# Recurrent attention and a Strassen-tiled MLP: one transfer per seventh of w_out, block 1's turns behind the step, the last output's sums inside its last products

## The chip, the cores and the metric

The kernel runs on one NeuronCore of a Trainium2 chip. The metric is device time in microseconds (us) of one execution; a figure given for a kernel is the median of several executions, and all outputs are float32.

## The reference

Attention in its recurrent form feeds a two-layer MLP with the quick-GELU gate:

```python
# q, k, v: (4, 8, 768, 64)
for t in range(S):
    state = gamma * state + einsum('bhd,bhe->bhde', k[:, :, t], v[:, :, t])
    y[:, :, t] = scale * einsum('bhd,bhde->bhe', q[:, :, t], state)
x = y.transpose(0, 2, 1, 3).reshape(3072, 512)
h = x @ w_in                                # 512 x 2048
g = h * (1.0 / (1.0 + exp(-1.702 * h)))
out = g @ w_out                             # 2048 x 512
```

gamma is one constant per head. The weights arrive as float64 words and are narrowed to float32 on the chip.

## The kernel before

**Blocks.** The 3072 rows are worked in six blocks (`for m in range(NB)`) of 512. Attention runs in 24 chunks of 64 time steps for two batches each; four chunks make the x of a block. Chunk j is made by three functions. `turn(j)` brings its q and k into the transposed form (from chunk 8 on by VectorE's transposes, L251) and then starts the loads of chunk j + 2 (16 transfers on SP's queue, L154). `step(j, f)` lets TensorE work on chunks j and f at once: L287 multiplies k and q of chunk j into `pa`, L295 makes the state's update, L304 and L310 the output `py` of chunk f. VectorE then masks `pa` into `at` (L316), updates the state (L366), makes `tmp` (L328) and the block's x in `X` or `X1` (L345); POOL scales k into `kd` (L272) and ages the state (L357). `pa` and `py` have one buffer each, so a step can't start before VectorE has read the step before.

**Products.** `up` makes h from x and w_in, `down` and `down49` make the output from g and w_out. Matrix products follow the Strassen-Winograd scheme: seven products of half-size quarters instead of eight, with sums of quarters before and after. Blocks 0 and 1 use this once for w_out (`down`, matmuls on L684: 28 units `n`, eight recorded matmuls each, of seven products with four units). Blocks 2 to 5 use it once in `up` (L469) and twice in `down49` (L572): each of the seven products is again seven products of quarters of quarters, here called the seven inner products of each *seventh*.

**What is prepared during blocks 0 and 1.** While TensorE works on blocks 0 and 1, the other engines make the sums that later blocks need:
- `inner_w2(i)`, VectorE, once per seventh i: three sums of w_out's quarters (L519) into `X[:, 4]`, `X[:, 5]`, `X[:, 6]`, each built on the one before, and for each a transfer on SP's queue (L520) into the DRAM tile `W2D[i]`, from where `stream` (L541) brings them back on POOL's queue in blocks 2 to 5. All seven sevenths use the same three slots of X, so a slot can be written again only when its transfer has read it. These slots hold part of block 0's g before, and the sums of x for block 2 after: `sums_x` (POOL, L440 to L443) makes `X[:, 4]`, `X[:, 6]`, `X[:, 5]` and `X[:, 2]` at the end of block 1, and the third product of `up` reads `X[:, 5]`.
- `inner_w2_t3` (L525), one more sum per seventh, in place.
- `sums_w1` (POOL, L432 to L435), sums of w_in; two tiles of 1792 KB of them leave on SP's queue to DRAM (L437, `W1D`).
- `sums_g(m, p)`: VectorE's L456, L457, L458 and POOL's L459 make sums of g between the third and the fourth product of `down`; the fourth product (units 12 to 15) reads them.

**Order.** Only TensorE's order, and some early work, is kept as written. For the other engines a scheduler orders the instructions when the program is built, from the order in which they are recorded and from what they depend on; each engine and each queue then runs its own in that order, and an instruction that waits holds all behind it. In block 1 the list `between` hands one entry to the recording after every third unit: the decay of chunk 8 with the loads of k and v, then `step` 9, `turn` 10, `step` 10, `turn` 11, and so on to `step` 12, one entry each. From block 2 on an entry is a step together with the next turn.

**Outputs.** `put` (L658 in `down`, L589 in `down49`) sums a finished product with kept ones into `o` and sends it out: in `down` on POOL's queue (L661), in the last block on ACT's (L602). In `down49` each of a block's four output tiles takes a first sum for each of the two halves of a seventh's inner products (L593, 128x512 and 128x384) and four more that put the inner products together (L598 to L601). For the very last output these follow the last matmul of the kernel.

Of the kernel before, what the change touches and what calls it, by code (L numbers as in the profile page):

```python
# [9 lines left out]
F32 = mybir.dt.float32  # L10
# [3 lines left out]
P = 128  # L14
# [14 lines left out]
def kernel(  # L29
# [29 lines left out]
    pe, act, dve, pool, sp = nc.tensor, nc.scalar, nc.vector, nc.gpsimd, nc.sync  # L59
# [8 lines left out]
    CB = 4  # L68
    BT = CB * P
    TH = BT // 2  # L70
    NB = NCH // CB
# [12 lines left out]
    ps = ctx.enter_context(tc.tile_pool(name="ps", bufs=2, space=bass.MemoryType.PSUM))  # L84
# [428 lines left out]
    def inner_w2(i):  # L513

        b11, b12, b21, b22 = w2q(ORDER[i][1])
        t = []
        for k, a in enumerate((b12, b22, b21)):
            t.append(X[:, 4 + k].rearrange("p c (d e) -> p (c d) e", e=P))
            dve.tensor_sub(t[k], a, t[k - 1] if k else b11)  # L519
            sp.dma_start(W2D[i][:, k], t[k])  # L520

    def inner_w2_t3(i):

# [25 lines left out]
    def down49(m, ring, comps):  # L549

        b, t0 = m * CB // NC * 2, m * CB % NC * D
        rows = out.rearrange("(b t) (e c) -> e t b c", b=B, c=EH)[:, t0:t0 + TH, b:b + 2, :] \
            .rearrange("e (h p) b c -> h e p b c", p=P)
        own = late.tile([P, 7, 4, P], F32, name="own", tag="late1")
        acc, kept = {}, {}

        def derive(i):
            q = [G[:, u::2, ORDER[i][0], h * P:(h + 1) * P] for u in range(2) for h in range(2)]
            a11, s3, a12, s2 = q
            d = own[:, i % 2 * 3:i % 2 * 3 + 3]  # L560
            dve.tensor_add(d[:, 0], s2, a11)
            dve.tensor_sub(d[:, 1], a12, s2)
            dve.tensor_add(d[:, 2], s2, s3)
            b11, t3, b21, b22 = w2q(ORDER[i][1])
            t1, t2, t4 = [comps[i][:, k] for k in range(3)]
            return [(a11, b11), (a12, b21), (s2, t2), (s3, t3)], [(d[:, 0], t1), (d[:, 1], b22), (d[:, 2], t4)]

        def products(p0, pairs, new):
            for j in ((0, 1, 3, 2) if len(pairs) == 4 else range(3)):
                a, w = pairs[j]  # L570
                for d in range(NP // 2):
                    pe.matmul(p0[:, j, :], a[:, d], w[:, d], start=(new and j == 0 and d == 0),  # L572
                              stop=(d == NP // 2 - 1), skip_group_check=True)

        def home2(name, first, rest):
            kept[name] = first.rearrange("p (j e) -> p j e", e=P), rest[:, 0:3 * P].rearrange("p (j e) -> p j e", e=P)
            return kept[name]

        flat = X[:, 4:6].rearrange("p s c t -> p (s c t)")
        def keep(name, half):  # L580
            if half == 0:
                if name in "pt":
                    home2(name, flat[:, 0:4 * P], flat[:, 4 * P:7 * P])
                else:
                    home2(name, (own if name == "u" else ring)[:, 6].rearrange("p j e -> p (j e)"),
                          one.tile([P, 2 * EH], F32, name=name, tag="s2" if name == "u" else "s3"))
            return kept[name][half]

        def put(th, e, half, y, a):  # L589
            if half == 0:  # L590
                kept[th, e] = two.tile([P, 7, P], F32, name="o")
            c = kept[th, e]
            dve.tensor_add(c[:, 4 * half:4 + 3 * half], y, kept[a][half])  # L593
            if half == 0:
                return
            last = m == NB - 1
            eng = dve if last else pool
            eng.tensor_add(c[:, 1:3], c[:, 1:3], c[:, 0:1].to_broadcast([P, 2, P]))  # L598
            eng.tensor_add(c[:, 3], c[:, 3], c[:, 2])
            eng.tensor_add(c[:, 0:5:4], c[:, 2:4], c[:, 4:5].to_broadcast([P, 2, P]))  # L600
            eng.tensor_add(c[:, 2:4], c[:, 0:4:3], c[:, 5:7])  # L601
            (act if last else pool).dma_start(rows[th, e], c[:, 1:5].rearrange("p (b f) e -> p b (f e)", b=2))  # L602

        def then(i, half, p0):
            if i == 0:
                act.activation(keep("p", half), p0, AF.Copy)
            elif i == 1:
                put(0, 0, half, p0, "p")
            elif i == 2:
                act.activation(keep("u", half), p0, AF.Copy)  # L610
            elif i == 3:
                act.activation(keep("v", half), p0, AF.Copy)
            elif i == 4:
                u = kept["u"][half]
                dve.tensor_add(keep("t", half), p0, u)
                put(1, 1, half, p0, "v")
            elif i == 5:
                put(0, 1, half, p0, "t")
            else:
                put(1, 0, half, p0, "v")  # L620

        pairs = {}
        todo = []
        for i in range(7):
            for half in range(2):
                def unit(i=i, half=half):
                    if half == 0:
                        if i == 0:
                            pairs[0] = derive(0)
                        x = "x" if i in (0, 2, 3) else "y"  # L630
                        if i != 2 and i != 3:
                            for n in range(2):
                                acc[x, n] = ps.tile([P, 4 - n, P], F32, name="pq", tag=x)
                    x = "x" if i in (0, 2, 3) else "y"
                    products(acc[x, half], pairs[i][half], i not in (2, 3))
                    then(i, half, acc[x, half])
                    if half == 0 and i < 6:
                        pairs[i + 1] = derive(i + 1)
                    if half == 1:
                        if i + 2 < 7:  # L640
                            comps[i + 2] = stream(ring, i + 2)
                        if i in (0, 1, 3):
                            sums_g_outer((0, 1, None, 2)[i])
                todo.append(unit)
        return todo
# [189 lines left out]
    """.split():  # L835
        works[name]()
    ordered[0] = False
    def chunks(first, last):

        return [s for j in range(first, last + 1)  # L840
                for s in (lambda j=j: turn(j), lambda j=j: step(j, j - 1))]

    for m in range(NB):
        between = []
        if m == 0:
            between = [lambda: turn(2 * CB), lambda: step(2 * CB), lambda: None, lambda: None, lambda: turn(2 * CB + 1)]
        elif m == 1:
            between = [lambda: (decay(2 * CB), load(2 * CB + 1, "v"))] + chunks(2 * CB + 1, 3 * CB)[1:]
        elif 1 < m < NB - 1:
            last = min((m + 2) * CB, NCH - 1)  # L850
            for j in range((m + 1) * CB + 1, last + 1):
                between.append(lambda j=j: (step(j, j - 1), j < last and turn(j + 1)))
            if last == NCH - 1:
                between.append(lambda: step(None, NCH - 1))
        if m > 1:
            if m > 2:
                W1B[:] = [late.tile([P, 2, 7, 2, P], F32, name=f"W1B{i}", tag=f"late{i}") for i in range(2)]
                pool.dma_start(W1B[0], W1D[0])
            for d in range(NP // 2):
                up(d)  # L860
                if d == 0 and m > 2:
                    pool.dma_start(W1B[1], W1D[1])
                if d == 0 and m < NB - 1:
                    turn((m + 1) * CB + 1)
                if d == NP // 2 - 2:
                    ring = begin_ring()
                if m == 2:
                    for i in range(2 * d, min(7, 2 * d + 2)):
                        inner_w2_t3(i)
        for n, unit in enumerate(down(m) if m < 2 else down49(m, *ring)):  # L870
            unit()
            if m == 0 and n < NP and n % 2:
                sums_w2(n - 1)
            if m == 0 and NP <= n < 3 * NP // 2:
                sums_w2_t3(2 * (n - NP))
            if m == 1 and n % 8 == 3:
                sums_w1(n // 4)
            if m == 1 and n % 3 == 1 and n < 21:
                inner_w2(n // 3)
            if between and (n % 3 == 2 if m < 2 else n % 3 == 1):  # L880
                between.pop(0)()
                if m == 1 and not between:
                    sums_x()
            if 1 < m < NB - 1 and n == 11:
                sums_x()
# [46 lines left out]
```

## Time and profile before

| what | us |
|---|---|
| median of 6 executions | 675.34 |
| lowest, highest | 675.03, 676.61 |
| the profiled execution | 675.44 |
| its span, from the first to the last instruction | 673.7 |
| TensorE busy in it | 653.7 |
| VectorE busy | 442.3 |
| POOL busy | 170.7 |

The profile is one execution. Times in it count from the span's start. PE is TensorE, PEld its loading of weights, DVE VectorE, ACT ScalarE, POOL GpSimd, SP the engine that only issues transfers; a "q" behind a name is the engine's sequencer or queue. A row of a timeline gives start, length, engine, line, operation, output<-input, shapes, the number of instructions merged into it, and in brackets the idle time before it with what ended it. The share of the clock that TensorE was granted is 1.00 at full speed. A float32 matmul is recorded as two.

### The profile page before, as it was taken

The page shows a single profiled execution, that of the slowest core. Times are in us where ns is not written, and L with a number is a line of the kernel's source. Part 1 is how long each engine was busy: PE and PEld are TensorE (multiplying, and loading weights), DVE is VectorE, ACT ScalarE, POOL GpSimd, SP SyncE. Part 2 cuts the span into 40 slices and gives each one's busy share as a digit, 9 for nine tenths or more (in the row PEclk, how much of TensorE's full clock was granted, in tenths as well). Part 3 has the DMA queues.
Part 4 walks back from the last instruction along what each step waited for, and adds up shares of the span by engine and source line. Part 5 has one row for each costly group of instructions (what it writes and reads, how often), then busy time and mean ns, then how long its engine had stood idle before and what let it go on. Part 6 is the DMA issues. An engine that isn't in the chain of part 4 may idle for free.

```text
span 673.7 us, 15357 instructions
## 1 busy us (share of the span) xinstructions
PE 653.7 (97%) x6502; PEld 568.5 (84%) x6502; DVE 442.3 (66%) x613; ACT 156.7 (23%) x313; POOL 170.7 (25%) x189
## 2 busy tenths in 40 slices
PE   6799999999999899999999999999999999999996
PEld 4688864747888778888999988999988999988996
DVE  3798890879868795254986254996254995254964
ACT  5665423321000000233210233110233110233110
POOL 3000000020278241300245700255700255400000
PEclk9999999999999979999999999999999999999999
DMA  9989741332324944322177662276662243602232
GB/s 184 219 221 224 190 135 70 133 94 44 67 86 149 331 115 113 86 31 94 61 177 176 187 171 94 66 180 174 184 169 93 67 142 110 250 0 94 69 136 95
DMA packets 145493, 88.98 MB, mean 132 GB/s; under 512 B 129648, under 2 KB 130672, under 8 KB 144400
## 3 DMA queue, kind: packets, MB, share of 16 engines
q1 hardware_dynamic: 136528, 48.27, 31.1%
q0 software_dynamic: 6752, 38.42, 15.8%
q10 hardware_dynamic: 2144, 1.31, 0.7%
q8 instruction: 51, 0.84, 0.5%
q14 instruction: 18, 0.15, 0.1%
HBM read 72.37 MB, written 15.47 MB: 130 GB/s over the span
## 4 chain that ended last, share of the span: by engine, by line
PE 87%; DVE 5%; DMA 4%; issue 2%; POOL 1%; SPq 0%; ACT 0%; POOLq 0%; DVEq 0%; ACTq 0%
PE pq L572 26%; PE px L469 16%; PE py L469 12%; PE ph L425 8%; PE pd L684 8%; PE ph L412 8%; DVE X L519 2%; PE pa L287 2%; DMA W2D<-X 2%; PE py L310 2%; PE pa L295 1%; PE py L304 1%; PE pt L248 1%; DMA v_in<-in_v_dram 1%; DMA whole<-in_col_decay_dram 1%
## 5 line engine op out<-in xcount | busy, mean ns | idle before, releaser
L572 PE MATMUL pq<-W,G 128*128 128x128 f32 x672 | 80.2, 276 | 0.0
L572 PEld LDWEIGHTS pq<-W,G 128*128 128x128 f32 x672 | 77.6, 192 | 1.2 <-issue 0.7
L541 POOL DMA_DIRECT2D ring<-W2D x28 | 15.5, 554 | 232.2 <-PE px L469 121.9
L469 PE MATMUL px<-X,W1A 128*128 128x256 f32 x256 | 59.8, 379 | 0.0
L469 PE MATMUL px<-X,W1B 128*128 128x256 f32 x256 | 59.8, 379 | 0.0
L572 PE MATMUL pq<-ring,own 128*128 128x128 f32 x448 | 59.8, 276 | 0.0
L572 PEld LDWEIGHTS pq<-ring,own 128*128 128x128 f32 x448 | 54.5, 192 | 0.4
L469 PEld LDWEIGHTS px<-X,W1B 128*128 128x128 f32 x256 | 48.6, 190 | 6.6
L469 PEld LDWEIGHTS px<-X,W1A 128*128 128x128 f32 x256 | 48.4, 190 | 6.5
L684 PE MATMUL pd<-W,G 128*128 128x256 f32 x224 | 50.6, 386 | 0.0
L684 PEld LDWEIGHTS pd<-W,G 128*128 128x128 f32 x224 | 43.0, 194 | 6.2
L469 PE MATMUL py<-X,W1B 128*128 128x256 f32 x192 | 45.4, 379 | 0.0
L469 PE MATMUL py<-X,W1A 128*128 128x256 f32 x192 | 45.4, 379 | 0.0
L391 ACT ACTIVATE G<-G 128x512 f32<-128x512 f32 x48 | 30.2, 630 | 52.0 <-DVE G L479 33.3
L469 PEld LDWEIGHTS py<-X,W1B 128*128 128x128 f32 x192 | 36.5, 190 | 5.0
L469 PEld LDWEIGHTS py<-X,W1A 128*128 128x128 f32 x192 | 36.5, 190 | 5.0
L487 DVE TENSOR_TENSOR t<-py,u 128x512 f32<-128x512 f32 x16 | 11.1, 692 | 35.5 <-PE py L469 35.5
L476 ACT ACTIVATE p<-px 128x512 f32<-128x512 f32 x16 | 9.6, 597 | 96.7 <-PE px L469 96.7
L572 PE MATMUL pq<-W,own 128*128 128x128 f32 x224 | 29.6, 275 | 0.0
L572 PE MATMUL pq<-ring,G 128*128 128x128 f32 x224 | 29.6, 275 | 0.0
L501 DVE TENSOR_TENSOR G<-G 128x512 f32<-128x512 f32 (+2 forms) x24 | 12.3, 513 | 25.7 <-ACT G L391 25.7
L412 PE MATMUL ph<-X,W1A 128*128 128x256 f32 x128 | 29.1, 383 | 0.0
(196 smaller groups left out, 1185.7 us busy)
## 6 DMA issues: line engine op xcount, KB each, us to landing
ring<-W2D POOLq DMA_DIRECT2D x28, 768.0 KB, 4.9
W1B<-W1D POOLq DMA_DIRECT2D x6, 1792.0 KB, 10.3
W<-in_moe_w_in_dram SPq DMA_DIRECT2D x12, 512.0 KB, 7.1
W2D<-X SPq DMA_DIRECT2D x21, 256.0 KB, 2.8
W<-in_moe_w_out_dram SPq DMA_DIRECT2D x10, 512.0 KB, 4.2
out_dram<-o POOLq DMA_DIRECT2D x20, 256.0 KB, 3.6
v_in<-in_v_dram SPq DMA_DIRECT2D x64, 64.0 KB, 3.2
q_sq<-in_q_dram SPq DMA_DIRECT2D x128, 32.0 KB, 2.2
```

The lines of the kernel that those rows point to most:

```text
L287: pe.matmul(pa[HALF[w], u, 0, s, :], kt[HALF[u], w, s, :], qt[HALF[u], w, s, :], start=True, stop=True)
L310: pe.matmul(py[HALF[o], w, 0, 2 * u + s2 if f < 2 * CB else 2 * s2 + u, :], vn[HALF[w], HP * u + s, :], a[HALF[w], u, s, :], start=True, s ...
L391: pin(act.activation(g, h[:, i], AF.Gelu_apprx_sigmoid))
L412: pe.matmul(h[:, ab], w, X[:, 2 * th + c // 2, c % 2, :], start=(ab == 0 and c == 0), stop=(c == 3), skip_group_check=True)
L425: pe.matmul(h, w, X1[:, c // 2:4:2, c % 2, :], start=(c == 0), stop=(c == 3))
L469: pe.matmul(acc[:, u, :], t[:, q1 + u, sa, c, :], X[:, sb, c, :], start=(start and u == 0 and c == 0), stop=(stop and c == 1), skip_group_ ...
L487: dve.tensor_add(tt, z, u)
L501: dve.tensor_sub(q[0][1], q[0][0], q[0][1])
L519: dve.tensor_sub(t[k], a, t[k - 1] if k else b11)
L541: pool.dma_start(c, W2D[i])
L572: pe.matmul(p0[:, j, :], a[:, d], w[:, d], start=(new and j == 0 and d == 0), stop=(d == NP // 2 - 1), skip_group_check=True)
L684: pe.matmul(p0[:, n, :], g1(m, p, sa)[:, n * P:(n + 1) * P], W2[:, sb, p, :], start=(new and p == 0 and n == 0), stop=(last and p == NP - ...
```

## The change

It has three parts.

1. `inner_w2` makes its three sums as before and then issues one transfer of all three slots (768 KB) instead of one of 256 KB after each sum.
2. In block 1, an entry of `between` is now a step with the next turn, followed by an empty entry. The steps stay behind the same units; the turns of chunks 10, 11 and 12 are recorded right behind the step before them, three units earlier.
3. The last inner half-product of the last block goes through the new `finish`: its first product gets the old accumulator `p0`, the other two a tile `p1` of their own. The five sums that need only `p0` and kept values are recorded ahead of one last sum that needs `p1`, and the output leaves in four transfers of 64 KB, three on ACT's queue and one on SP's, each behind the sum that completes it.

The matmuls are the same, in the same order. In the built program the scheduler's order on the other engines differs in blocks 0 and 1 too: on VectorE, the mask, the state's update, the transposes of turn 10 and the step's two output sums of step 9 stand behind the fifth seventh, and three sums of the sixth seventh ahead of the sums of g; on SP, the transfers of the sixth and the seventh seventh stand behind the loads of turns 11 and 12; on POOL, the third output transfer of block 1 stands ahead of the four sums of `sums_x` instead of behind them, and `X[:, 6]` ahead of `X[:, 5]`.

```diff
@@ inner_w2
         for k, a in enumerate((b12, b22, b21)):
             t.append(X[:, 4 + k].rearrange("p c (d e) -> p (c d) e", e=P))
             dve.tensor_sub(t[k], a, t[k - 1] if k else b11)
-            sp.dma_start(W2D[i][:, k], t[k])
+        sp.dma_start(W2D[i].rearrange("p k d e -> p (k d e)"), X[:, 4:7].rearrange("p k c t -> p (k c t)"))
@@ products, in down49
-            for j in ((0, 1, 3, 2) if len(pairs) == 4 else range(3)):
+            for j in ((0, 1, 3, 2) if len(pairs) == 4 else range(len(pairs))):
@@ new, in down49
+        def finish(p0, ab):
+            c, v = kept[1, 0], kept["v"][1]
+            p1 = ps.tile([P, 2, P], F32, name="pq", tag="x")
+            products(p0, ab[:1], True)
+            products(p1, ab[1:], True)
+            at = [rows[1, 0][:, b, f * P:(f + 1) * P] for b in range(2) for f in range(2)]
+            dve.tensor_add(c[:, 1:3], c[:, 1:3], c[:, 0:1].to_broadcast([P, 2, P]))
+            act.dma_start(at[0], c[:, 1])
+            dve.tensor_add(c[:, 3], c[:, 3], c[:, 2])
+            dve.tensor_add(c[:, 4], p0[:, 0], v[:, 0])
+            dve.tensor_add(c[:, 0:5:4], c[:, 2:4], c[:, 4:5].to_broadcast([P, 2, P]))
+            act.dma_start(at[3], c[:, 4])
+            dve.tensor_add(c[:, 5:7], c[:, 0:4:3], v[:, 1:3])
+            dve.tensor_add(c[:, 2:4], p1, c[:, 5:7])
+            for n in range(2):
+                (act, sp)[n].dma_start(at[1 + n], c[:, 2 + n])
@@ unit, in down49
+                    if i == 6 and half == 1 and m == NB - 1:
+                        finish(acc[x, half], pairs[i][half])
+                        return
                     products(acc[x, half], pairs[i][half], i not in (2, 3))
@@ main loop; chunks() is removed
         elif m == 1:
-            between = [lambda: (decay(2 * CB), load(2 * CB + 1, "v"))] + chunks(2 * CB + 1, 3 * CB)[1:]
+            between = [lambda: (decay(2 * CB), load(2 * CB + 1, "v"))]
+            for j in range(2 * CB + 1, 3 * CB + 1):
+                between += [lambda j=j: (step(j, j - 1), j < 3 * CB and turn(j + 1)), lambda: None]
+            between.pop()
```

More of the change, by code (lines that the diff above doesn't have):

```diff
@@ L837 @@
     ordered[0] = False
-    def chunks(first, last):
-        return [s for j in range(first, last + 1)
-                for s in (lambda j=j: turn(j), lambda j=j: step(j, j - 1))]
     for m in range(NB):
```

## The prediction

> **What bounds the kernel now.** I read the page first, for the engine that is never idle, then the chain of waits around its one hole, then the engines' timelines there and at the end.
>
> ```profile
> span 673.7 us, 15357 instructions
> ...
> PE 653.7 (97%) x6502; PEld 568.5 (84%) x6502; DVE 442.3 (66%) x613; ACT 156.7 (23%) x313; POOL 170.7 (25%) x189
> ...
> PEclk9999999999999979999999999999999999999999
> ```
>
> TensorE is busy all through; the only dent in its clock is slice 15 (236 to 253 us), in block 1. The chain there, columns start, length, what:
>
> ```profile
> 207.92 7.31 DVE X L519
> ...
> 221.48 7.39 DMA W2D<-X
> ...
> 228.96 1.29 DVE X L519 x2
> ...
> 236.03 0.62 DVE qT L251
> 236.65 0.60 DVE kT L251
> 237.26 0.14 issue
> 237.39 1.21 PE pa L287 x25
> ```
>
> The transposes of turn 10 (L251) stood late in VectorE's order, behind the sums of w_out's quarters (L519), one of which took 7.31 us beside POOL, and a wait of 7.39 us for their transfer. TensorE idled 4.08 us, to 237.39, and then worked at half clock (window, PE, PEld, DVE, ACT, POOL busy, clock, DMA share, GB/s):
>
> ```profile
> 221.00:233.00 12.00, 12.00 (x169) 10.65 (x160) 7.22 (x11) 0.57 (x1) 2.81 (x3) 1.00 1.01 371
> ...
> 237.40:243.30 5.90, 5.90 (x133) 5.42 (x134) 5.90 (x8) 0.00 (x0) 2.86 (x3) 0.50 0.53 122
> ...
> 15.00:27.00 12.00, 7.27 (x270) 6.30 (x267) 9.15 (x16) 8.31 (x23) 0.67 (x2) 1.00 1.06 203
> ```
>
> A step takes 2.03 us elsewhere and took 3.70 here; the next 48 matmuls took 11.69 us against 10.63. The hole costs 4.08 + 1.67 + 1.06 = 6.8 us. The first window shows the transfer queue full at 371 GB/s just before. The start of block 2, on TensorE and then POOL:
>
> ```profile
> 273.86 1.89 PE L469 MATMUL px<-X,W1A 128*128 128x256 f32 x8
> ...
> 277.31 1.89 PE L469 MATMUL px<-X,W1A 128*128 128x256 f32 x8
> ```
>
> ```profile
> 270.73 1.27 POOL L442 TENSOR_TENSOR X<-X 128x512 f32<-128x512 f32 x1
> ...
> 273.30 1.72 POOL L443 TENSOR_TENSOR X<-X 128x512 f32<-128x512 f32 x1
> ```
>
> The product at 277.31 reads X[5], which L442 makes by 272.0: 5.3 us to spare. The end, on VectorE and on ACT's queue:
>
> ```profile
> 668.41 0.56 DVE L593 TENSOR_TENSOR o<-pq,v 128x384 f32<-128x384 f32 x1 [1.20 <-PE pq L572]
> 669.00 0.42 DVE L600 TENSOR_TENSOR o<-o 128x256 f32<-128x256 f32 x1
> 669.46 0.42 DVE L601 TENSOR_TENSOR o<-o 128x256 f32<-128x256 f32 x1
> ```
>
> ```profile
> 669.91 0.38 ACTq L602 DMA_DIRECT2D out_dram<-o  x1
> ```
>
> Prices of transfers (KB each, us to landing):
>
> ```profile
> W2D<-X SPq DMA_DIRECT2D x2, 256.0 KB, 2.0
> ```
>
> ```profile
> W1D<-W1B SPq DMA_DIRECT2D x1, 1792.0 KB, 6.5
> ```
>
> ```profile
> ring<-W2D POOLq DMA_DIRECT2D x28, 768.0 KB, 4.9
> ```
>
> **One transfer per seventh.** 21 issues on SP become 7; SP's time was waiting, so the 14 issues of 0.32 us saved are worth nothing. But the first sum of the next seventh rewrites X[4], which now waits for 768 KB that leave after the third sum, where it waited for 256 KB that left after the first. So sums and transfer of successive sevenths stand in series. A transfer of 768 KB is not shown from SP; between 2.0 us (256 KB) and 4.9 us (the same size read back by POOL) I take the line through 2.0 and 6.5 us: 2.0 + 512/1536 x 4.5 = 3.5 us. A sum alone follows the last by 0.70 us; beside POOL's sums of w_in it takes 1.49 to 1.76, and I take 1.65. The first seventh ends at 195.56 as before. Seventh 1: 199.1 to 204.1; 2: 207.6 to 212.5; 3: 216.0 to 220.6 (POOL's sums end near 219.8). The two 1792 KB transfers of w_in's sums follow POOL: the first enters the queue at about 216.4, ahead of seventh 3's, the second behind it, and seventh 4's behind both. From 217.2, 1.0 us after that issue (the landing of 2.0 us less its data), the queue must move 1792 + 768 + 256 (an output) + 1792 + 768 KB = 5.5 MB: at 371 GB/s 14.8 us, so the fifth transfer lands at 232.2. At the 449 GB/s of the best slices in that stretch it is 230.0; at 4.9 us a transfer, sevenths 1 to 3 are 4.2 us later and it lands near 235. Meanwhile seventh 4's sums run at about 225.1 to 227.2.
>
> **Turns behind the step.** In the changed program's order on VectorE, mask, state, both transposes of turn 10, and the step's two output sums follow seventh 4 directly: six instructions, 3.7 us, done at 230.9. TensorE asks for them at 232.9, so its wait is gone, with 2 us of cover; seventh 4 later than 229.2 brings it back. turn's loads of q and k move with it on SP: in the changed order the 16 of turn 11 (some 9 us of issues, as from 249.6 to 259.0 before, and held until its transposes near 248) stand ahead of the sixth transfer, so that this is issued near 257 and lands near 260.5. The last seventh's first sum stands in VectorE's order near 257 and holds it up to 3.5 us; behind it wait only sums due after TensorE's unit that ends near 264, so I cost this at nothing. The last transfer, behind eight loads of k and v (5.1 us) and the 16 of turn 12 (8.0), is issued near 270.5 and lands near 274.0; L440, which overwrites its source, could not start before 275 anyway (below), a cover of 1 us.
>
> What is late next are the block's own sums of G (L456 to L458), 12 instructions, which now stand behind the sixth seventh. They begin after the fifth landing and five VectorE sums: 232.2 + 5 x 0.61 = 235.3. They take 12 x 0.60, 8 dependent ones 0.1 more (0.8), and three subtractions of POOL's (L459, 1.26 less the overlap, 1.13 each: 3.4): 11.4 us, ending 246.7. TensorE's fourth unit after the step reads the last. Before, that unit began at 252.6 - 3 x 1.73 = 247.4; without any stall it would be 240.5. So of 6.8 us the stage keeps 0.7, between 2.9 (landing at 230.0) and -2.1 (235).
>
> **The start of block 2.** In POOL's order the block's third output transfer stood behind the four sums of X (L440 to L443); in the changed order it stands ahead of them, and X[5] comes third instead of second. That output is the last product of block 1. Counted from TensorE's end of the block (273.86 before): VectorE's sum ends 0.9 us later, POOL starts the issue 0.3 later (221.15 after 220.86 in the trace), 0.74 to issue, three sums 3.75: X[5] comes 5.7 us after the block's end, and its product wants it at 3.45. TensorE stalls 2.3 us. With the 0.7 kept, the stage ends 1.6 us late (-0.6 to +4.4).
>
> **The end.** Before, three VectorE sums end 1.50 us after the last matmul, at 669.88. After, the others run during the last products (L593 to 666.4, then five of 0.29 or 0.42 with 0.03 between, to 668.2) and one 128x256 sum of 0.42 is left: 668.84, 1.04 us earlier. 64 KB on each of two queues instead of 256 KB on one: 2.16 us to landing becomes 1.95 (q's 32 KB loads land in 1.9 to 2.2). Together -1.25 us, between -0.9 and -1.5.
>
> Sum: +1.6 - 1.25 = +0.35. The profiled execution took 675.44 us around its span of 673.7, 0.1 over the median of 675.34; so 675.7.
>
> [...] Before, one sum was held 7.30 us, through five POOL instructions. [...]
>
> [...] Idling of 1.80 us at 24.48 left the clock at 1.00 (third window above), 4.08 did not. Stalls of 2.3 are nearer the first, so I add nothing, and keep 3 us (half of the 5.9 us window at 0.50) as the other end.
>
> **Rivals.**
> - Exchange (forecast, chance 0.44): the hole goes, two smaller ones come, the end gains. 675.7, own range 674.2 to 676.6.
> - The queue is quick (0.26): fifth landing at 230.0 to 230.5, for which the best slices speak, against it the 371 GB/s of the whole window. Stage -0.6, end -1.25 to -1.5: -1.85 to -2.1, so 673.2 to 674.0.
> - Slow transfers in series (0.20): fifth landing at 235, for which the 7.39 us above speaks, and against it the 2.0 us of an empty queue. +4.4 - 1.25 = +3.15: 678.5. It decides from a landing of 233.2 on, each us costing one.
> - Half clock after the new stalls (0.10): for it, 6 us of idling in pieces within 12 us; against it 24.48. +0.35 + 3 = 678.8.
>
> 0.2%, 1.35 us, is about what a measurement of this kernel can tell. The quick case and a little of the exchange's edge make faster 0.28, the exchange same 0.41, the last two slower 0.31. The range reaches from the quick case's end to just above the slow one, and leaves some 0.1 on either side.
>
> **What would show it.** No wait of L287 on kT near 233; waits of the 128x256 matmuls for L458 between 236 and 246; a wait for L442 at the start of block 2; W2D landings of 3.5 us and, behind W1D, more; the last VectorE sum 0.45 us after the last matmul. I am wrong if the sums of G do not wait for the fifth landing, or if X[5] is ready in time.

## The result, and the profile after

The change made the kernel slower. The median went from 676.33 us (67 executions) to 680.13 us (30); the ratio of the paired executions is 1.0052, 95% interval 1.0044 to 1.0061, so +3.5 us. The forecast was 675.7 us, +0.35. The ratios below leave out two executions far above the others of their kernels (695.16 us of the kernel without the end, 848.81 us of the one called g7_three_act).

Every profile holds TensorE's 6502 records in the same order, so the n-th is the same matmul in all of them. Subtracting its start in the profile of before from its start in another shows how far behind that one is there, and the steps between are the stages. "Start" runs to 200 us, "block 1" to the first product of block 2 (273.86 before), "block 2" to that block's fourth (279.04), "later" to the last matmul, "end" from there to the span's end, which is known to 0.1 us (us against before):

```
                 start  block 1  block 2  later   end    span
after            +1.54   -1.23    +5.70   +0.45  -1.96   +4.5
```

The start is scatter: two profiles below, with equal orders up to block 1, differ there by 4.4 us. Leave it out and the change is +3.0 by the profile, near the +3.5 measured.

Block 1 went as meant. Line numbers shift with the edits: L684 of before is L705 here (L706 in the last kernels below), L660 and L661 are L681 and L682, and L469 becomes L470 in the last kernels. TensorE's timeline of the changed kernel around step 10 and after it:

```profile
234.78 0.69 PE L287 MATMUL pa<-qT,kT 64*64 64x64 f32 x32
...
238.97 1.97 PE L705 MATMUL pd<-W,G 128*128 128x256 f32 x8 [2.10 <-DVE G L458]
241.88 1.99 PE L705 MATMUL pd<-W,G 128*128 128x256 f32 x8 [0.94 <-DVE G L458]
245.36 1.99 PE L705 MATMUL pd<-W,G 128*128 128x256 f32 x8 [1.49 <-DVE G L458]
```

Step 10 (L287) waits for nothing: the hole is gone. Three new waits for the sums of G, 4.5 us, give most of it back; the clock stays at 1.00 through them. On VectorE the last idle time ahead of those sums is a wait for the fifth transfer:

```profile
233.68 0.69 DVE L519 TENSOR_TENSOR X<-W 128x512 f32<-128x512 f32 x1 [1.87 <-DMA W2D<-X]
...
236.69 0.69 DVE L456 TENSOR_TENSOR G<-G 128x512 f32<-128x512 f32 x1
```

The loss is at the third product of block 2. TensorE there, then POOL:

```profile
281.56 3.65 PE L469 MATMUL px<-X,W1A 128*128 128x256 f32 x8 [3.78 <-POOL X L442]
```

```profile
275.36 0.73 POOL L682 DMA_DIRECT2D out_dram<-o  x1 [5.19 <-DVE o L681]
277.81 1.26 POOL L440 TENSOR_TENSOR X<-X 128x512 f32<-128x512 f32 x1 [1.72 <-DMA W2D<-X]
279.03 1.25 POOL L441 TENSOR_TENSOR X<-X 128x512 f32<-128x512 f32 x1
280.25 1.25 POOL L442 TENSOR_TENSOR X<-X 128x512 f32<-128x512 f32 x1
```

The third output is issued by 276.09, but L440 starts only at 277.81: it waits for the last seventh's transfer, whose source it overwrites. TensorE then idles 3.78 us, and the product takes 3.65 us instead of 1.89, since the clock has fallen, to 0.53. Windows of both stretches (PE, PEld, DVE, ACT, POOL busy, clock, DMA share, GB/s):

```profile
277.00:281.50 4.50, 0.78 (x4) 0.35 (x2) 0.69 (x1) 0.63 (x1) 3.69 (x3) 1.00 0.67 168
281.56:285.20 3.64, 3.64 (x9) 2.98 (x10) 0.00 (x0) 0.00 (x0) 1.26 (x1) 0.53 0.05 11
```

Why the transfer is late is on SP's timeline:

```profile
258.39 0.45 SPq L520 DMA_DIRECT2D W2D<-X  x1
258.94 3.21 SPq L140 DMA_DIRECT2D kn_in<-in_k_dram  x4
262.25 2.57 SPq L140 DMA_DIRECT2D v_in<-in_v_dram  x4
264.92 4.92 SPq L154 DMA_DIRECT2D q_sq<-in_q_dram  x8
269.94 4.02 SPq L154 DMA_DIRECT2D k_sq<-in_k_dram  x8
274.06 0.39 SPq L520 DMA_DIRECT2D W2D<-X  x1
```

Its last sum on VectorE begins at 267.11 and takes 0.68 us:

```profile
267.11 0.68 DVE L519 TENSOR_TENSOR X<-W,X 128x512 f32<-128x512 f32 x1
```

The issue comes 6.3 us after that, behind the 16 loads of turn 12, which the second part of the change moved ahead. In the kernel before, the last transfers of the last seventh stood ahead of these loads:

```profile
264.29 1.08 SPq L520 DMA_DIRECT2D W2D<-X  x2
265.47 4.47 SPq L154 DMA_DIRECT2D q_sq<-in_q_dram  x8
```

The chain of waits of the changed kernel runs through the landing:

```profile
274.06 3.60 DMA W2D<-X
...
277.81 1.26 POOL X L440
279.06 1.22 POOL X L441
280.29 1.23 POOL X L442
281.52 0.04 issue
281.56 3.65 PE px L469 x8
```

The chain's row ahead of these is a sum of L525 that ends as the issue begins. The transfer does not depend on it: the issue follows the last load at 0.10 us, as between the other rows above, and in a kernel below it left at 273.99 while that sum was still running.

The transfers themselves, and the end, on VectorE:

```profile
W2D<-X SPq DMA_DIRECT2D x7, 768.0 KB, 3.6
```

```profile
674.23 0.43 DVE L635 TENSOR_TENSOR o<-o,v 128x256 f32<-128x256 f32 x1
674.86 0.42 DVE L636 TENSOR_TENSOR o<-pq,o 128x256 f32<-128x256 f32 x1 [0.21 <-PE pq L572]
```

One sum is left behind the last matmul, as forecast.

### The profile page after: what moved, and what is told of

It reads as the page before. It is cut to its first block, busy times and chain, and to the rows that moved or that the text cites. A ratio compares the mean times of both kernels' runs of the same rounds, so it can differ in the third digit from the quotient of the medians.

```text
span 678.2 us, 15331 instructions
## 1 busy us (share of the span) xinstructions
PE 654.9 (97%) x6502; PEld 568.0 (84%) x6502; DVE 437.9 (65%) x614; ACT 157.1 (23%) x313; POOL 169.8 (25%) x189
## 3 DMA queue, kind: packets, MB, share of 16 engines
q10 hardware_dynamic: 2304, 1.25, 0.6%
## 4 chain that ended last, share of the span: by engine, by line
PE 91%; DVE 4%; DMA 3%; POOL 1%; SPq 0%; issue 0%; POOLq 0%
PE pq L572 26%; PE px L469 16%; PE pd L705 12%; PE py L469 12%; PE ph L425 8%; PE ph L412 8%; PE pt L248 2%; PE pa L287 2%; PE pa L295 2%; PE py L310 2%; PE py L304 1%; DMA kn_in<-in_k_dram 1%; DMA v_in<-in_v_dram 1%; DMA q_in<-in_q_dram 1%; DVE G L457 1%; DVE G L458 1%
## 5 line engine op out<-in xcount | busy, mean ns | idle before, releaser
L469 PE MATMUL px<-X,W1A 128*128 128x256 f32 x256 | 61.6, 387 | 3.8 <-POOL X L442 3.8
L469 PE MATMUL px<-X,W1B 128*128 128x256 f32 x256 | 59.8, 379 | 0.0
L469 PEld LDWEIGHTS px<-X,W1A 128*128 128x128 f32 x256 | 49.3, 194 | 11.1 <-POOL X L442 4.2
L705 PE MATMUL pd<-W,G 128*128 128x256 f32 x224 | 50.4, 382 | 4.8 <-DVE G L458 4.8
L469 PEld LDWEIGHTS px<-X,W1B 128*128 128x128 f32 x256 | 48.6, 190 | 6.6
L705 PEld LDWEIGHTS pd<-W,G 128*128 128x128 f32 x224 | 42.0, 190 | 11.8 <-DVE G L458 3.9
L469 PE MATMUL py<-X,W1A 128*128 128x256 f32 x192 | 45.4, 379 | 0.0
L469 PE MATMUL py<-X,W1B 128*128 128x256 f32 x192 | 45.4, 379 | 0.0
L469 PEld LDWEIGHTS py<-X,W1A 128*128 128x128 f32 x192 | 36.6, 191 | 5.0
L469 PEld LDWEIGHTS py<-X,W1B 128*128 128x128 f32 x192 | 36.5, 190 | 5.0
```

The source lines that it names most:

```text
L469: pe.matmul(acc[:, u, :], t[:, q1 + u, sa, c, :], X[:, sb, c, :], start=(start and u == 0 and c == 0), stop=(stop and c == 1), skip_group_ ...
L705: pe.matmul(p0[:, n, :], g1(m, p, sa)[:, n * P:(n + 1) * P], W2[:, sb, p, :], start=(new and p == 0 and n == 0), stop=(last and p == NP - ...
```

## The experiments

The theories. **A**: the last seventh's transfer stands on SP's queue behind the loads of turn 12, and block 2's sums of x wait for its landing. **B**: what holds the sums of x is the third output transfer ahead of them on POOL. A and B can both be true: L440 starts when the later of the two is over. **C**: single transfers in series with the sums cost by themselves. D, E and F came with the later runs. The stages of all profiles, and the measured ratios to before with their 95% intervals:

```
                      start  block 1  block 2  later   end    ratio
e1_finish             +0.51   -0.34    +0.00   +1.04  -1.50   0.9986 (0.9975-0.9997)
e2_one                +0.82   +1.10    +0.00   +0.04  -0.56   1.0027 (1.0018-1.0036)
e3_turns              +1.06   -0.71    +1.27   +0.11  +0.06   1.0028 (1.0010-1.0046)
e4_one_turns          +0.71   -1.25    +5.69   +0.59  -0.33   1.0072 (1.0056-1.0087)
g1_last_on_act        +1.47   -1.27    +0.00   -0.18  -1.92   0.9972 (0.9958-0.9986)
b1_third_output_act   +1.85   -1.25    +4.82   +0.94  -1.66   1.0048 (1.0031-1.0065)
h3_turn10             +1.89   -0.69    +0.00   +0.58  -1.58   0.9969 (0.9956-0.9983)
g7_three_act          +1.66   +0.53    +0.00   -0.04  -1.35   0.9965 (0.9948-0.9982)
k1_g_first            +0.24   -6.89    +2.48   -0.26  -1.87   0.9973 (0.9959-0.9988)
k1_second_look        +2.11   -6.89    +3.54   +0.16  -1.92   (one execution)
k2_g_first_three      +4.66   -6.89    +0.00   -0.20  -1.28   0.9900 (0.9880-0.9920)
k3_g_first_no_turns   +1.01   +1.09    +0.00   -0.13  -1.37   1.0009 (0.9996-1.0022)
```

### The parts alone

**The end alone** (e1_finish): the kernel before with `finish` and its call.

```diff
+        def finish(p0, ab):
...
+                    if i == 6 and half == 1 and m == NB - 1:
+                        finish(acc[x, half], pairs[i][half])
+                        return
```

> The third part of the change alone (the last output's sums inside its last products); w_out's transfers and the turns as before. The profile after shows 3.37 us from TensorE's last matmul to the span's end, where before there were 5.33. All theories about block 1 leave this part alone: it should be worth 1.3 to 2.0 us, so 0.2 to 0.3 % faster than before. A rival reading is that the end of the profiled execution was merely a lucky one and the fourfold output is worth nothing: then the same as before.

Measured: -0.14%, 0.9 us (0.2 to 1.7). The end is 1.50 us shorter in the profile; in the three kernels without the third part it varies by 0.6 us (-0.56 to +0.06). Worth something near 1 us, under the expected 1.3 to 2.0, into which its interval reaches.

**One transfer alone** (e2_one): before with

```diff
-            sp.dma_start(W2D[i][:, k], t[k])
+        sp.dma_start(W2D[i].rearrange("p k d e -> p (k d e)"), X[:, 4:7].rearrange("p k c t -> p (k c t)"))
```

> The first part alone (one transfer per seventh), turns and end as before. Theory A (the last seventh's transfer stands on SP's queue behind the loads of turn 12, and block 2's sums of x wait for its landing): in this kernel the last transfer stands ahead of those loads, so it lands well before block 1 ends, no sum of L440 waits for it, and the time is within 2 us of before; the wait of step 10 for its transposes near 233 stays. Theory B (the third output transfer ahead of the sums of x on POOL): it stands behind them here, so also within 2 us. Theory C (single transfers in series with the sums are dear by themselves): later sevenths delay the transposes of turn 10 and the sums of G more than before, 3 to 5 us slower.

Measured: +0.27%, 1.8 us. The hole at step 10 grew from 4.08 to 5.47 us, as the transposes still stand behind a sum that now waits longer for its transfer (3.20 us, 1.83 before):

```profile
239.59 1.14 PE L287 MATMUL pa<-qT,kT 64*64 64x64 f32 x32 [5.47 <-DVE kT L251]
```

No stall in block 2, and within 2 us of before, as both A and B say; C's 3 to 5 us did not come. Series costs here, but 1 to 2 us. With the transposes moved ahead it costs nothing that block 1 shows: -1.23 with single transfers against -0.71 with three (turns alone, below).

**Turns alone** (e3_turns): the kernel before with

```diff
-            between = [lambda: (decay(2 * CB), load(2 * CB + 1, "v"))] + chunks(2 * CB + 1, 3 * CB)[1:]
+            between = [lambda: (decay(2 * CB), load(2 * CB + 1, "v"))]
+            for j in range(2 * CB + 1, 3 * CB + 1):
+                between += [lambda j=j: (step(j, j - 1), j < 3 * CB and turn(j + 1)), lambda: None]
+            between.pop()
```

> The second part alone (turns directly behind the step), three transfers per seventh and the end as before. The hole of 6.8 us at step 10 should go. Theory A: the three transfers of the last seventh stand behind the loads of turn 12 as in the changed kernel, but the first sums are free earlier with transfers of 256 KB, so that the landing comes near 270 to 272 and delays L440 by at most 1 us: 1 to 4 us faster than before. Theory B (POOL's third output ahead of the sums of x decides): block 2 stalls by 2 to 4 us at its third product here too, and at most 1 us is gained. Theory C: as A, since there is nothing in series here.

Measured: +0.28%, 1.9 us (0.7 to 3.1). No theory had it right. The profile shows the hole gone and the same kind of stalls for the sums of G as with single transfers:

```profile
238.41 1.96 PE L684 MATMUL pd<-W,G 128*128 128x256 f32 x8 [2.01 <-DVE G L458]
241.32 1.99 PE L684 MATMUL pd<-W,G 128*128 128x256 f32 x8 [0.95 <-DVE G L458]
245.40 1.99 PE L684 MATMUL pd<-W,G 128*128 128x256 f32 x8 [2.09 <-DVE G L458]
278.84 1.99 PE L469 MATMUL px<-X,W1A 128*128 128x256 f32 x8 [1.00 <-POOL X L442]
```

So 5.05 us of the hole come back there without any series. The last seventh's first transfer was issued at 272.87, also behind the loads of turn 12, and the last at 273.9; by the median of 2.2 us from issue to landing in this profile I put the last landing near 276.1, an estimate, where A had expected 270 to 272. But it is not a landing that L440 waits for here. POOL:

```profile
275.41 0.72 POOL L661 DMA_DIRECT2D out_dram<-o  x1 [6.50 <-DVE o L660]
276.16 1.28 POOL L440 TENSOR_TENSOR X<-X 128x512 f32<-128x512 f32 x1
277.52 1.27 POOL L442 TENSOR_TENSOR X<-X 128x512 f32<-128x512 f32 x1
```

L440 follows the third output without idle time; the slot that it overwrites was free when the first of the three transfers had landed, by the same estimate near 275.1. So in this kernel the output ahead of the sums of x is the last wait, as B has it, and the 1.00 us of TensorE, less than B's 2 to 4, is about what it delayed L440 (275.1 to 276.16). Of the measured 1.9 us the stages explain 0.7; the rest stays open.

**Both, without the end** (e4_one_turns): the changed kernel without `finish`:

```diff
-                    if i == 6 and half == 1 and m == NB - 1:
-                        finish(acc[x, half], pairs[i][half])
-                        return
```

> The first and second part without the third. Every theory: the changed kernel without its gain at the end, so slower than before by the 3.5 us of the change plus 1.3 to 2.0 us, some 5 to 5.5 us, with the stall of 3.8 us and the half clock at the third product of block 2 as in the changed kernel. If the three parts do not add up (this kernel at or below the changed one), the cost lies in what the third part does to the order elsewhere.

Measured: +0.72%, 4.9 us, just under the expected 5 to 5.5. The stall of 4.16 us is there, and the product behind it takes 3.29 us for 1.89. The stages of block 1 and block 2 are those of the changed kernel to 0.02 us, so the third part does nothing to them. The large loss in block 2 needs the first two parts together: 5.7 us, where either alone has 0.0 and 1.3.

### Which queue

**The last transfer on ACT's queue** (g1_last_on_act): the changed kernel with

```diff
-        sp.dma_start(W2D[i].rearrange(
+        (act if i == 6 else sp).dma_start(W2D[i].rearrange(
```

> The changed kernel with one edit: the last seventh's transfer is issued on ACT's queue, so it no longer stands behind the loads of turn 12 on SP's. In the built program the third output transfer of block 1 then falls behind the four sums of x on POOL. Theory A (the place of that transfer on SP's queue is what cost): it goes as soon as the last sum is made (267.8 in the changed kernel's profile), lands near 271.4, L442 ends before its product asks for X[5], and the stall of 3.78 us and the half clock's 1.7 us both go: 5.5 us under the changed kernel, about 2 us or 0.3 % under the kernel before. Theory B (the third output ahead of the sums of x decides): the same here, since that output moves too; the next run tells them apart. Theory C (single transfers in series cost in block 1): at most 1 us of the change's 3.5 comes back.

Measured: 0.28% under before (0.14 to 0.42), 1.9 us, and 0.8% under the changed kernel. The last sum begins at 266.5 and takes 0.7 us, and L440's wait for the landing ends at 271.93, near the 271.4 that A said. POOL:

```profile
271.93 1.26 POOL L440 TENSOR_TENSOR X<-X 128x512 f32<-128x512 f32 x1 [2.32 <-DMA W2D<-X]
273.15 1.25 POOL L441 TENSOR_TENSOR X<-X 128x512 f32<-128x512 f32 x1
274.38 1.71 POOL L442 TENSOR_TENSOR X<-X 128x512 f32<-128x512 f32 x1
```

X[5] is ready at 276.09 and its product runs at 277.51 without a wait; block 2's 5.70 us are gone, and block 1 is as it was. One transfer's queue turned the change from a loss into a gain, with what the scheduler made of it: the third output, too, now stands behind the sums of x, so this run by itself does not tell A from B.

**The third output on ACT's queue** (b1_third_output_act): the changed kernel with

```diff
-            (pool if m < NB - 1 else act).dma_start(rows[th, e], o)
+            (act if m == NB - 1 or (m == 1 and (th, e) == (0, 1)) else pool).dma_start(rows[th, e], o)
```

> The changed kernel with one edit: the third output transfer of block 1 is issued on ACT's queue, so that on POOL nothing stands between the second output and the sums of x; the last seventh's transfer stays on SP behind the loads of turn 12. Theory A: L440 waits for the landing near 277.7 exactly as in the changed kernel; within 0.5 us of it, 3.5 us slower than before, with the stall of 3.8 us and the half clock. Theory B: the stall falls to at most 1 us, no half clock, so 4 to 5 us under the changed kernel and 0.5 to 1.5 us under before.

Measured: +0.48%, 3.2 us: within 0.5 us of the changed kernel. POOL was free for 7.61 us and L440 still waited for the landing:

```profile
277.61 1.26 POOL L440 TENSOR_TENSOR X<-X 128x512 f32<-128x512 f32 x1 [7.61 <-DMA W2D<-X]
```

```profile
281.37 3.30 PE L469 MATMUL px<-X,W1A 128*128 128x256 f32 x8 [3.29 <-POOL X L442]
```

So in the changed kernel the landing is the last wait, as A says, and taking the output away alone gains nothing: L440 could not start anyway. It does not follow that the output costs nothing. In the changed kernel POOL was free of it at 276.09; three sums from there, 3.70 us, would end near 279.8, and TensorE was ready for the product at 277.78. With the landing in time and the output still ahead, some 2.0 us of the 3.78 would be left. That is an estimate from these rows, and no run has that pair with a single transfer; the turns alone come nearest. What the runs show is that the late landing alone is enough for the stall (3.29 us here), that the output alone costs 1.00 us with the turns alone, and that the edit of one transfer's queue removes both.

**Turn 10 alone behind its step** (h3_turn10), three transfers, and the end:

```diff
-            between = [lambda: (decay(2 * CB), load(2 * CB + 1, "v"))] + chunks(2 * CB + 1, 3 * CB)[1:]
+            between = [lambda: (decay(2 * CB), load(2 * CB + 1, "v")), lambda: (step(2 * CB + 1, 2 * CB), turn(2 * CB + 2)),
+                       lambda: None] + chunks(2 * CB + 2, 3 * CB)[1:]
```

> Of the second part only turn 10 follows its step; turns 11 and 12 stand where they stood before, so their loads stay behind the sixth and the seventh seventh on SP's queue. Three transfers per seventh as before, and the third part. Theory A: the hole at step 10 goes, the stalls for the sums of G stay (some 5 us for a hole of 6.8), and no sum of x is late, so block 2 begins 1 to 2 us early; with the end's 1 to 2 us it is 2 to 4 us faster than before (0.3 to 0.6 %). Theory D (the stalls for the sums of G give back all of the hole): only the end's gain is left, 1 to 1.5 us faster.

Measured: 0.31% under before (0.17 to 0.44), 2.1 us. The last seventh stands ahead of turn 12's loads again: L440, at 270.59, waited 0.84 us for VectorE's L345 and for no landing, and block 2 has no stall. The stalls for the sums of G stay (2.02, 0.95 and 2.08 us); block 1 keeps 0.69.

**All turns and the end, three transfers, the last seventh's on ACT's queue** (g7_three_act): the changed kernel with

```diff
+            (act if i == 6 else sp).dma_start(W2D[i][:, k], t[k])
-        sp.dma_start(W2D[i].rearrange("p k d e -> p (k d e)"), X[:, 4:7].rearrange("p k c t -> p (k c t)"))
```

> The second and third part, with three transfers per seventh as before, those of the last seventh on ACT's queue. Theory A: all turns may follow their steps as long as the last seventh leaves in time: no wait at the third product of block 2, the hole gone, the stalls for the sums of G of some 5 us kept: 2 to 4 us faster than before, like the kernel with turn 10 alone. Theory B: the third output behind the sums of x as a consequence gives the same. Theory D: 1 to 1.5 us faster.

Measured: 0.35% under before (0.18 to 0.52), 2.4 us, like turn 10 alone, as A has it, and B too, since the output stands behind the sums here. D's figure, 1 to 1.5 us, reaches into both intervals, so the times alone don't exclude it; by the profile of turn 10 alone block 1 keeps 0.69, so the stalls give back most of the hole and not all. In the profile of this one block 1 is 0.53 longer than before: the clock was at 0.50 behind the same stalls (shown at the end).

### What is left in block 1

**Sums of G first** (k1_g_first), on the kernel with the last transfer on ACT's queue:

```diff
     def sums_g(m, p):
+        first = tc.keep_in_program_order if m == 1 else lambda i: i
         a = [g(m, p, s) for s in range(4)]
-        dve.tensor_add(a[3], a[2], a[3])
+        first(dve.tensor_add(a[3], a[2], a[3]))
...
-            dve.tensor_sub(t[k], a, t[k - 1] if k else b11)
+            (tc.keep_in_program_order if i > 3 else lambda i: i)(dve.tensor_sub(t[k], a, t[k - 1] if k else b11))
```

The other two sums of `sums_g` get the same `first`.

> The kernel with the last seventh's transfer on ACT's queue (turns behind the steps, one transfer per seventh, sums inside the last products), and VectorE's order held so that block 1's sums of G stand ahead of the fifth, sixth and seventh seventh. Theory E (what is left in block 1 is VectorE's order: sums that wait for a transfer stand ahead of the sums of G): the three stalls of 2.06, 0.94 and 1.48 us for L458 go, 4.5 us; the last three sevenths come later, and the last landing may hold L440 by 1 to 2 us: 2.5 to 4.5 us under that kernel, so 4.5 to 7 us (0.7 to 1.0 %) under before. Theory F (the sums of G are bounded by VectorE's and POOL's own work from the step on, whatever stands ahead): the stalls stay within 1 us of their 4.5, and the time within 1 us of that kernel, 2 us under before.

Measured: 0.27% under before, no better than without the order, although the profile has block 1 at -6.89 us: no stall in it at all. E is right on block 1, wrong on the time. The sevenths are later, POOL stands idle for 7.23 us before L440, to 269.28, and block 2 waits 2.21 us. The row of L440 names no releaser; the last sum ends at 265.48, and with 3.6 us for a transfer of 768 KB the landing comes near 269.1, so I take it for the wait, an estimate. Its executions spread from 669.5 to 676.0 us, and a second profile was taken of the same kernel.

> The kernel with the sums of G first and one transfer per seventh, run once more for a second profile: the first profiled execution took 669.52 us, where the median of its executions was 674.48. If the difference is the start of the kernel, which differed by up to 4.4 us between profiled executions with the same orders there, block 1 and block 2 look as in the first profile (block 1 6.9 us shorter than before, one stall of 2.2 us at the third product of block 2). If it is the landing of the last seventh, that stall is 3 us or more in an execution near 674 and half clock follows it.

Measured: 672.86 us, 3.3 above the first profile. Block 1 is the same; 1.9 us are the start, and 1.1 are in block 2, with a shorter wait and the clock at 0.57 behind it, where the first profile has 1.00. That product's line in the first profile, and in the second:

```profile
273.04 1.99 PE L470 MATMUL px<-X,W1A 128*128 128x256 f32 x8 [2.21 <-POOL X L442]
```

```profile
274.67 3.34 PE L470 MATMUL px<-X,W1A 128*128 128x256 f32 x8 [1.97 <-POOL X L442]
```

Neither expected alternative holds whole, and what takes other executions to 676 is open.

**The same order with three transfers** (k2_g_first_three), on the kernel with all turns, three transfers and the last seventh's on ACT's queue (the diff is the same):

> The same order on VectorE with three transfers per seventh, those of the last on ACT's queue. Theory E: all stalls of block 1 go (2.06, 0.95 and 2.09 us, and the 1.3 us of half clock that followed them in the profile of that kernel without the order), and as a transfer of 256 KB lands 1.4 us sooner than one of 768 KB, the sums of x for block 2 are in time: 5 to 6.5 us under that kernel, 7 to 8.5 us (1.0 to 1.25 %) under before. Theory F: within 1 us of that kernel, 2 us under before.

Measured: 669.29 us, 1.0% under before (0.8 to 1.2), 6.8 us; the best of all kernels run, and just under E's 7 to 8.5. It has the second and the third part of the change, and not the first: with this order, one transfer per seventh (0.9973) is worse than three (0.9900). From step 10 on TensorE runs through:

```profile
239.93 10.63 PE L706 MATMUL pd<-W,G 128*128 128x256 f32 x48
250.49 0.69 PE L287 MATMUL pa<-qT,kT 64*64 64x64 f32 x32
...
264.63 7.17 PE L706 MATMUL pd<-W,G 128*128 128x256 f32 x32
271.64 1.89 PE L470 MATMUL px<-X,W1A 128*128 128x256 f32 x8
...
275.09 1.89 PE L470 MATMUL px<-X,W1A 128*128 128x256 f32 x8
```

**The same order without moving the turns** (k3_g_first_no_turns), on the kernel with the end alone (the same diff again):

> The kernel before with the third part and the same order on VectorE (sums of G ahead of the last three sevenths); turns where they were, three transfers on SP's queue. Theory E in its strong form (the hole of 6.8 us at step 10 and the stalls for the sums of G have one cause, sums of sevenths that wait for their transfer ahead of urgent work on VectorE): the transposes of turn 10 are no longer behind such a sum, the hole goes without any turn being moved, 5 to 7 us from it and 1 to 2 us at the end, so 6 to 8.5 us (0.9 to 1.25 %) under before. Weak form (the turns must be moved for the hole): the hole of 4 us and its half clock stay, and only the end's 1 to 2 us are gained.

Measured: 1.0009 (0.9996 to 1.0022), the same as before, which neither form had. The hole at step 10 went, as the strong form says, but a new one came at the next step that meets sums of sevenths ahead of its transposes:

```profile
266.13 1.13 PE L287 MATMUL pa<-qT,kT 64*64 64x64 f32 x32 [6.64 <-DVE kT L251]
```

On VectorE the transposes of turn 12 follow the last sum of the last seventh there, at 264.69. So both belong together: turns early, and sums of sevenths behind the sums of G.

## Why the prediction was wrong, point by point

Times of the changed kernel are put on before's base by taking off the 1.54 us of its start.

- **The failed step** is the last transfer: "issued near 270.5 and lands near 274.0; L440 ... could not start before 275 anyway, a cover of 1 us". It was issued at 272.5 and landed at 276.1. The issue of the sixth transfer near 257 was right (256.9). From there to the last I had 5.1 + 8.0 us of loads, and they took 5.9 (258.94 to 264.82) + 9.0 (264.92 to 273.96), with 0.55 more for the sixth transfer's own issue. The term was short by 2 us, and the cover I had named was 1; POOL was free for L440 at 274.55 besides, not at 275, since block 1 ended 0.5 us sooner than forecast. So L440 waited 1.72 us for the landing. Before's own rows gave the warning: the three groups of 16 loads in block 1 took 10.1, 9.3 and 8.5 us. I took a price under all three for the step whose cover was the thinnest.
- **The stall at the start of block 2** came out 3.78 us instead of 2.3. I put all of it on the third output ahead of the sums of x. That output was issued when forecast (1.2 us after the block's end at 274.17), and by the rows it alone would have left some 2.0 us (the estimate above). But the landing ended later and was what L440 waited for: that is the other 1.7, and with the output off POOL the stall stayed, at 3.29. A wait that I had counted as covered stood behind the one that I priced.
- **The half clock** after it I gave a chance of 0.10 and no place in the sum. It cost 1.8 us (3.65 for 1.89). The stalls of 2.10 and less in block 1 left the clock at 1.00, as I had it; behind the one of 3.78 it was 0.53. Whether one of 2.3 there would have is not shown, as stalls near 2 us came out both ways in other kernels (below). The two errors came together, and a stage that is 1 us short of its cover pays more than that 1 us.
- **Right:** step 10's wait goes; the fifth seventh lands at 232.1 (forecast 232.2); sums of G begin at 235.2 (235.3) and block 1 keeps 1.2 us (0.7); a transfer of 768 KB takes 3.6 us (3.5); one sum is left at the end. The end itself was 1.96 us shorter in that profile (1.25 forecast; 1.28 to 1.96 in all profiles with the third part, where those without it vary by 0.6).
- **Right, but not the whole reason:** I had the sums of G wait for the fifth landing, and in the changed kernel they do (the 1.87 us above). But with three transfers per seventh (turns alone) they begin at the same time, 236.13 less 1.06 = 235.07, behind a run of sums without idle time. That they stand behind the sums of the sevenths at all is VectorE's order; with them ahead of the last three the stalls go. The sum for that landing was also added wrongly, by little: 217.2 + 14.8 is 232.0 and not 232.2, and at 449 GB/s it is 229.5 and not 230.0.
- **The sum:** -1.2 + 5.7 + 0.45 - 1.96 = +3.0 against my +1.6 - 1.25. Of the 2.6 us between, block 2 has 3.4 (5.70 for 2.3): 1.5 are the longer stall, 1.8 its half clock, and 0.1 to 0.2 the distance between products that the stall's figure leaves out. Block 1, the end and the later stages come to -0.7 together (-0.5, -0.7, +0.45).
- **The rivals:** "slow transfers in series" gave +3.15 us, close to the measured time by luck, and is not what happened: its deciding landing of 233.2 or later did not come. "Half clock after the new stalls" is nearest, behind a longer stall than those it named.

## What to carry to other kernels

When a block of work is moved ahead in one queue, count what is pushed back behind it there and follow each to whoever overwrites its source: here 16 small loads, some 9 us of issues, stood between a finished sum and the transfer that freed its buffer. A cover of 1 us under a chain of 15 us of issues is no cover; put the transfer on a queue that is idle. Where two things stand ahead of the same instruction, only the later one shows in the profile as its wait (here 1.72 us for the landing, and none for the output that ended at 276.09): price both, since removing one leaves the other. And in a stage that is already short of slack, removing one hole only shows the next wait of the same cause: look for the instruction that waits ahead of urgent work, not for the work that is late.

## What the runs showed of the hardware

- **An idle stretch of the same length may or may not cost the clock.** Stalls of 2.0, 0.95 and 2.1 us in block 1 left it at 1.00 in two kernels and halved it in a third with the same stalls. Windows behind the last of them, of the kernel with turn 10 alone (clock 1.00) and of that with all turns and three transfers (0.50):

```profile
247.50:250.60 3.10, 2.81 (x14) 2.15 (x13) 3.10 (x5) 0.00 (x0) 3.10 (x4) 1.00 0.38 86
```

```profile
247.50:250.60 3.10, 3.10 (x8) 2.19 (x7) 3.10 (x5) 0.00 (x0) 3.10 (x4) 0.50 0.41 90
```

  One kernel lost it after 1.97 us (0.57 behind them) and kept it after 2.21 (1.00). Behind idle stretches of 3.29, 3.78, 4.08 and 5.47 us it was 0.58, 0.53, 0.50 and 0.50, and behind one of 4.16 a product took 3.29 us for 1.89. What decides it for stalls near 2 us is not shown.
- **One VectorE sum takes 7.3 us in every kernel with three transfers per seventh and in none with one.** The group of L519 in the kernel before and in the changed one (duration min/median/max in ns):

```profile
L519 DVE TENSOR_TENSOR X<-W,X x14: 644/824/7300, 193.1 to 249.9; 128x512 f32<-128x512 f32 x14
```

```profile
L519 DVE TENSOR_TENSOR X<-W,X x14: 679/693/1755, 194.7 to 267.1; 128x512 f32<-128x512 f32 x14
```

  The longest was 7.29 to 7.30 us in all seven kernels with three transfers, and at most 1.81 us in the six with one. The forecast knew the one row of before and took 1.65 us for a sum beside POOL's sums of w_in; by the runs, the 7.3 goes with the three transfers. What starts it was not tried.
- The stretch up to 200 us differs by up to 4.7 us between profiled executions (k2_g_first_three against before) and by 1.9 us between the two of k1's kernel, one program: as much as the change moved, and more. A difference of spans between two profiles says little until that stage is taken off.
